# Seven block products instead of eight in the first product of token mixing, for three of four pairs of batches

## The chip, the cores and the metric

The kernel runs on one core of a Trainium2 chip. The core has TensorE (matrix products, written PE in the profile, its weight loads PEld), VectorE (DVE), ScalarE (ACT), GpSimd (POOL) and SyncE (SP, which here only issues DMAs). The engines run side by side, each through its own queue in order, and meet through semaphores. TensorE writes its results to PSUM, a memory of a few banks; everything else lives in SBUF, 128 partitions wide. The metric is the device time of one execution in microseconds (us); lower is better.

## The reference

Eight batches of 576 tokens. First an attention without softmax, then an MLP mixer:

```python
kv  = einsum('bhsd,bhde->...', k, v)          # per head, 64 x 64
o   = q @ kv
x   = o / rms(o) * g_norm                      # (8, 576, 512) after the heads are joined
...
xt  = x.transpose(0, 2, 1)
h   = maximum(xt @ w_tok1, 0) @ w_tok2         # token mixing: 576 -> 256 -> 576
u   = x + h.transpose(0, 2, 1)
out = u + maximum(u @ w_ch1, 0) @ w_ch2        # channel mixing: 512 -> 1536 -> 512
```

All of it is float32. The weights arrive as 64-bit floats and are rounded to 32 bits on the chip ("rounding" below). The change touches `xt @ w_tok1`, the first product of token mixing.

## The kernel before

The batches go in four **pairs**. For each pair the kernel computes attention (five groups of 128-token tiles, `X[pair, 0]` to `X[pair, 4]`: `X[pair, 0]` and `X[pair, 1]` are the 512 first tokens of the first batch, two tiles of 128 x 512 each, `X[pair, 2]` and `X[pair, 3]` those of the second, and `X[pair, 4]` the last 64 tokens of both) and then token mixing. After the last pair comes channel mixing, some 585 us in which seven block products stand for eight at two levels already.

Token mixing of a pair (`token_mixing`, L598) has two products. The first (`tok1`, L601) has four results, one PSUM bank each: `acc[side, t]`, for the two batches `side` of the pair and the two halves `t` of the 256 hidden columns. Each is a sum of four matmuls of 128 x 128 x 512 over the four token tiles, 16 in all, plus a remainder of 64 tokens (`tok1_rem`, L608, four matmuls on half of the array's rows). A ReLU on ScalarE then moves each bank to `h1[side][:, t]`. The second product (`tok2`, L625) makes nine tiles `u0` to `u8`. Where a tile was seeded, ScalarE has copied x into the bank beforehand and copies the sum back; otherwise VectorE adds the bank to x. POOL issues the DMAs that write u to memory.

The order of everything is written by hand as strings of step names (`middle`, `steady`, `last`, from L1385), which `play` (L1317) runs through, and each engine works in that order. Names that matter here:

- `a` attention matmuls, `q` squares (ScalarE), `g` gains (VectorE, from PSUM), `t` sums of squares (VectorE), `m r i` mean, root (ScalarE) and inverse; then x is scaled by `s` on ScalarE (eight small instructions), by `d` on VectorE or by `p` on POOL. Attention is played a pair ahead of mixing; a minus, as in `-d31`, means the pair before that: for attention steps the pair that is being mixed, for `-u8` and `-v8` the pair mixed before.
- `kv`, `e`: the small products k-transposed times v, and their copies.
- `h00` to `h11`: the four sums of `tok1`; `hr`: the remainder and the ReLUs; `z`: seeds; `u0` to `u8`: `tok2`.
- a number: so many rounding steps. A block of channel weights takes two scalings on ScalarE and clamp, shift and add (a custom instruction) on VectorE. In the last pair four sums of `w_ch1` (`mix_ch1`, L292, VectorE, 128 x 1536 each) stand between the fourth and the fifth step (L1442).
- `x`: transposes of finished u tiles on VectorE, `b`: their DMAs; `f`, `l`, `lq`: loads; `o`, `c`, `s`: weights and sums for channel mixing.

PSUM has a pool `h` of four banks, which `tok1`, the seeds and `tok2` take in turn. The tile `h1` has two buffers, so one for each side. The second side's first half of a pair, `X[pair, 3]`, is made last: its attention `a3` runs just before the pair's `tok1`, and its scaling (`-i3 -d31 -s30`) beside it.

The mixing of pair 0 lies in `middle`, of pairs 1 and 2 in `steady`, of pair 3 in `last`; `steady` also holds the attention of the next pair, `last` holds none. In `last` `u0` follows `hr` at once; in the others `a1` and two kv products lie between them.

Of the kernel before, what the change touches and what calls it, by code (L numbers as in the profile page):

```python
# [11 lines left out]
F32 = mybir.dt.float32  # L12
# [3 lines left out]
ALU = mybir.AluOpType  # L16
# [4 lines left out]
def kernel(  # L21
# [32 lines left out]
    nc = tc.nc  # L54
    P = 128
    B, S, DM = k.shape
# [4 lines left out]
    J, JJ, HF, Q = 4, 5, 64, 32  # L61
    LO = P * J
    assert D == 64 and DM == 512 and S == LO + HF and B % 2 == 0
    NC, NF, NTOK = DM // P, DCH // P, DTOK // P
# [6 lines left out]
    NU = B + 1  # L71
    NG = 1 + B // 2
    T = 2 * P
    assert B // 2 == 4
    EPS = 1e-6
    TOP = (2.0 - 2.0 ** -3 - 2.0 ** -23) * 2.0 ** -96

    def pool(name, bufs, side="left", stack=ctx, **kw):
        return stack.enter_context(tc.tile_pool(name=name, bufs=bufs, side=side,
                                                reuse_waits="tile", **kw))  # L80
# [34 lines left out]
    def do(f, *a, **kw):  # L115
        return lambda: f(*a, **kw)

    late = {}
# [4 lines left out]
    def dma(o, i, engine=nc.sync):  # L123
        keep(engine.dma_start(o, i))

    def tensor_add(o, a, b, op=ALU.add, engine=nc.vector):
        keep(engine.tensor_tensor(out=o, in0=a, in1=b, op=op))  # L127

    def relu(o, a):
        keep(nc.scalar.activation(o, a, AF.Relu))  # L130

    def copy(o, a):
        keep(nc.scalar.copy(o, a))  # L133

    def matmul(*a, **kw):
        keep(nc.tensor.matmul(*a, **kw))  # L136
# [120 lines left out]
    def get_ch2(f):  # L257

        def loads(raw):
            t = raw.rearrange("p (f n) w -> p f n w", f=2)  # L260
            rows = words(moe_w_ch2)[ts(f, 2 * P)].rearrange("(f p) n w -> f p n w", f=2)
            return [(t[:, i], rows[i]) for i in range(2)]

        dst = w_ch2[:, 2 * f // NS, ds(2 * f % NS, 2)]
        return block(2 * DM, loads, dst.rearrange("p f h n -> p (f h n)"), True)
# [117 lines left out]
    def x_of(pair, i):  # L383

        return X[pair, i // 2][:, i % 2]
# [209 lines left out]
        return steps  # L595


    def token_mixing(pair, seeds, aside=()):  # L598
        h1, acc = {}, {}

        def tok1(side, t, js=range(J)):  # L601
            if js[0] == 0:
                acc[side, t] = ps["h"].tile([P, DM], F32, name="ps_h", tag="h")
            for j in js:
                matmul(acc[side, t], lhsT=w_tok1[j // 2][:, j % 2, ts(t, P)],
                                 rhs=x_of(pair, side * J + j), start=(j == 0), stop=False)

        def tok1_rem():  # L608
            for t in range(NTOK):
                for side in range(2):  # L610
                    r = ds(side * HF, HF)
                    matmul(acc[side, t], lhsT=w_tok1r[r, ts(t, P)],
                                     rhs=x_of(pair, 8)[r], start=False, stop=True)
            for side in range(2):
                h1[side] = hp_.tile([P, NTOK, DM], F32, name="h1", tag="h1")
                for t in range(NTOK):
                    relu(h1[side][:, t], acc[side, t])

        def seed(i):


            acc[i] = ps["h"].tile([P, DM], F32, name="ps_u", tag="h")
            copy(acc[i], x_of(pair, i))

        def tok2(i):  # L625
            if i not in seeds:
                n = "o" if i in aside else "h"
                acc[i] = ps[n].tile([P, DM], F32, name="ps_u", tag=n)
            first = i not in seeds
            if i < 8:  # L630
                for t in range(NTOK):
                    matmul(acc[i], lhsT=w_tok2[:, t, ts(i % J, P)], rhs=h1[i // J][:, t],
                           start=(first and t == 0), stop=(t == NTOK - 1), skip_group_check=True)
            else:
                for t in range(NTOK):
                    for side in range(2):
                        matmul(acc[i][ds(side * HF, HF)], lhsT=w_tok2[:, t, LO:],
                               rhs=h1[side][:, t],
                               start=(first and t == 0), stop=(t == NTOK - 1), skip_group_check=True)
            x = x_of(pair, i)  # L640
            if first:
                tensor_add(x, acc[i], x)
            else:
                copy(x, acc[i])
            if i == 8:
                dma(u_rest[ts(pair, P)], x, nc.gpsimd)
                for side in range(2):
                    dma(out[2 * pair + side, LO:], x[ds(side * HF, HF)], nc.gpsimd)
            elif i % 2 == 1:
                dma(  # L650
                    u_rows(2 * pair + i // J)[ds((i % J - 1) * P, 2 * P)]
                    .rearrange("(t p) e -> p t e", p=P), X[pair, i // 2], nc.gpsimd)

        steps = {f"h{s}{t}": do(tok1, s, t) for s in range(2) for t in range(NTOK)}
        steps |= {f"h{s}{t}{j}": do(tok1, s, t, (j,)) for s in range(2) for t in range(NTOK) for j in range(J)}
        steps |= {f"z{i}": do(seed, i) for i in seeds}
        return steps | {"hr": tok1_rem} | {f"u{i}": do(tok2, i) for i in range(9)}


    xg, xt, uT = {}, {}, {}  # L660
# [656 lines left out]
    def play(lines, after={}, **stages):  # L1317

        for name in " ".join(lines).split():
            if name.isdigit():
                for _ in range(int(name)):
                    next(stages["rounding"], lambda: None)()
            elif name[0] == "-":
                stages["before"][name[1:]]()
            else:
                next(stages[s][name] for s in ("attention", "mixing", "more")
                     if name in stages.get(s, ()))()
# [3 lines left out]
    tok2 = [get_tok2(t) for t in range(NTOK)]  # L1333
    first_rows = [get_tok1_half(j) for j in range(2)]
    channel = ([get_ch1(c, f) for f in range(2) for c in range(NC)]
               + [get_ch2(f) for f in range(NF // 2)])
    dma(g_row, bass.AP(tensor=g_norm.tensor, offset=g_norm.offset, ap=[[0, 1], list(g_norm.ap[0])]), nc.gpsimd)
    load(0)
    first_rows[0][0]()
# [32 lines left out]
    def spread_g():  # L1372
# [12 lines left out]
    middle = [  # L1385
# [5 lines left out]
    steady = [[  # L1391
# [10 lines left out]

    attentions = [attention(0, ((0,), (1,), (2,), (3,), (4,)))]
    attentions += [attention(p, ((0, 1), (2, 4), (3,))) for p in range(1, B // 2)]
# [16 lines left out]

    more |= {f"j{n}": do(keep_warm, n) for n in (4, 5, 21)}
    more["gs"] = spread_g
    more |= {f"zk{side}{half}": do(spread_k, side, half) for side in range(2) for half in range(2)}
    more |= {f"zz{side}": do(zero_rows, side) for side in range(2)}
    play(start, attention=attentions[0], mixing=mixings[0], more=more)
    play(middle, attention=attentions[1], mixing=mixings[0], before=attentions[0],
         more=more, rounding=rounding)
    for n in range(1, B // 2 - 1):
        play(steady[n - 1], attention=attentions[n + 1], mixing=mixings[n], before=attentions[n] | {"u8": mixings[n - 1]["u8"]},  # L1430
             more=more, rounding=rounding)


# [2 lines left out]
    late["w2"] = pool("sums", 1, "left", once).tile([P, 3, 4, FQ], F32, name="w2")  # L1436
    late["u0"] = pool("u0", 1, "left", once)
    late["sv0"] = pool("sva", 4, "left", once)
    for i in range(2):
        fetch_once(i)  # L1440
    fill = [list(rounding), mix_ch1()]
    woven = fill[0][:4] + fill[1] + fill[0][4:]  # L1442

    last = [
        "h00 -i3 -d31 -s30 2 -d40 2 o0", "h01 2 o1", "h10 2 o3", "h11 2 o2", "hr z2 1 o4", "u0 z3 1 c0", "u1 z4 1 c1 o5", "u2 z5 c2",
        "u3 z6 1 c3 o6", "u4 z7 1", "u5 z8 1", "u6 1 s0", "u7 s1 s2", "u8 s3 s4"]
    parts1 = [f for o in ORDER1 for f in split(1, o)]
    more = {f"c{i}": f for i, f in enumerate(t_sums(lambda n: uT[0][:, SB[n]]))}
# [98 lines left out]
```

## Time and profile before

| | us |
|---|---|
| median of 3 runs (lowest to highest) | 770.39 (770.33 to 770.89) |
| the profiled execution: span from first to last instruction | 768.4 |
| what lies around the span (median less span) | 2.0 |
| PE busy | 762.0 (99%) |
| DVE busy | 644.5 (84%) |
| ACT busy | 279.5 (36%) |
| POOL busy | 112.8 (15%) |

The stages that the change touches, as start and end on TensorE, with the busy time of each engine in them:

| stage | us | PE | DVE | ACT | POOL |
|---|---|---|---|---|---|
| `tok1` and remainder, pair 1 | 70.15 to 87.28 | 17.13 | 16.49 | 8.31 | 2.41 |
| the same, pair 2 | 111.84 to 128.97 | 17.13 | 13.62 | 9.23 | 1.65 |
| the same, pair 3 | 151.19 to 167.04 | 15.85 | 15.33 | 8.78 | 2.40 |
| `tok2`, pair 3 | 167.04 to 182.84 | 15.80 | 14.16 | 10.88 | 3.00 |

The profiled execution has no time of its own beside its span, so the 2.0 us are taken from the median. A line of the timeline reads: start, length (both us), engine, line of the kernel, operation, output and input by the program's names, shape, and how many instructions were merged. A float32 matmul shows as two instructions, one for each of its two passes. What stands in brackets is idle time before the line and who ended it. TensorE's stages of pairs 1 and 2 include one attention group (64 small matmuls, some 1.1 us).

### The profile page before, as it was taken

What the parts mean: (1) busy time and instruction counts of PE and PEld (TensorE: products, weight loads), DVE (VectorE), ACT (ScalarE), POOL (GpSimd) and SP (SyncE); (2) the same over time, 40 slices, a digit from 0 to 9 for tenths busy, and PEclk for the clock granted to TensorE, in tenths of its full rate; (3) what the DMA queues carried; (4) which work ended last, traced back from release to release, by engine and by line L of the source; (5) the groups of instructions that cost most, each with busy time, mean ns of one, the idle gap of its engine ahead of it and who ended that gap; (6) DMA issues with size and microseconds to landing.
All of it is one profiled execution on the core that took longest, in us unless ns stands there. A gap on an engine that the chain in (4) does not pass through costs nothing.

```text
span 768.4 us, 12735 instructions
## 1 busy us (share of the span) xinstructions
PE 762.0 (99%) x4694; PEld 614.3 (80%) x4694; DVE 644.5 (84%) x956; ACT 279.5 (36%) x563; POOL 112.8 (15%) x125
## 2 busy tenths in 40 slices
PE   9999999999999999999999999999999999999997
PEld 8655555446888888888888888888888888888887
DVE  4868886997757779899968989997898997798996
ACT  3656666773210332512234241123352213325221
POOL 1003030204410000002240002042000227000204
PEclk9999999999999999999999999999999999999999
DMA  9999997599798795599998578999659889855679
GB/s 353 374 374 371 367 373 279 177 332 333 245 290 319 288 284 169 168 275 214 224 228 250 152 221 219 262 187 265 193 154 293 160 227 209 200 153 155 153 192 119
DMA packets 137981, 188.28 MB, mean 245 GB/s; under 512 B 48704, under 2 KB 95808, under 8 KB 135872
## 3 DMA queue, kind: packets, MB, share of 16 engines
q1 hardware_dynamic: 102240, 168.72, 69.1%
q0 software_dynamic: 34848, 18.36, 16.1%
q8 instruction: 38, 0.62, 0.3%
q10 hardware_dynamic: 832, 0.39, 0.2%
q14 instruction: 23, 0.19, 0.1%
HBM read 138.28 MB, written 49.15 MB: 244 GB/s over the span
## 4 chain that ended last, share of the span: by engine, by line
PE 96%; DMA 2%; DVE 1%; SPq 0%; ACT 0%; issue 0%; DVEq 0%
PE ps_d L136 28%; PE ps_b L136 19%; PE ps_a L136 19%; PE ps_u L136 8%; PE ps_h L136 8%; PE ps_v L136 5%; PE ps_c L136 3%; PE ps_w L136 2%; PE ps_kv L136 2%; PE ps_o L136 2%; DMA raw<-in_moe_w_tok_dram 1%; DMA v_in<-in_k_dram 1%; PE ps_r L136 0%; DVE x L494 0%; DVE ms L522 0%; DVE w_tok L211 0%
## 5 line engine op out<-in xcount | busy, mean ns | idle before, releaser
L136 PE MATMUL ps_d<-ui,w 128*128 128x256 f32 x504 | 118.6, 379 | 0.0
L136 PEld LDWEIGHTS ps_d<-ui,w 128*128 128x128 f32 x504 | 95.8, 190 | 13.0
L133 ACT COPY ps_d<-ps_a 128x768 f32<-128x768 f32 (+1 forms) x56 | 32.0, 572 | 199.9 <-PE ps_a L136 196.9
L127 DVE TENSOR_TENSOR v<-v,v 128x1536 f32<-128x1536 f32 (+2 forms) x70 | 103.2, 1482 | 0.3
L136 PE MATMUL ps_b<-sv,w 128*128 128x256 f32 x324 | 78.9, 379 | 0.0
L136 PE MATMUL ps_a<-v,w 128*128 128x256 f32 x324 | 78.7, 379 | 0.0
L1266 POOL DMA_DIRECT2D out_dram<-us x24 | 26.8, 1835 | 291.8 <-ACT p L133 286.5
L136 PEld LDWEIGHTS ps_b<-sv,w 128*128 128x128 f32 x324 | 61.2, 190 | 8.9 <-issue 0.6
L136 PEld LDWEIGHTS ps_a<-v,w 128*128 128x128 f32 x324 | 61.6, 190 | 8.4
L136 PE MATMUL ps_u<-h,w_tok 128*128 128x512 f32 (+1 forms) x160 | 64.7, 599 | 0.0
L136 PE MATMUL ps_d<-v,w 128*128 128x256 f32 x258 | 62.7, 379 | 0.0
L130 ACT ACTIVATE v<-v 128x768 f32<-128x768 f32 (+1 forms) x54 | 42.6, 822 | 55.1 <-DVE v L127 52.3
L136 PE MATMUL ps_h<-x,w_tok 128*128 128x512 f32 x128 | 57.6, 600 | 0.7 <-DVE w_tok L211 0.6
L1266 POOL DMA_DIRECT2D out_dram<-r x40 | 41.3, 1926 | 102.0 <-ACT p L133 80.3
L136 PE MATMUL ps_d<-sv,w 128*128 128x256 f32 x228 | 55.4, 379 | 0.0
L136 PEld LDWEIGHTS ps_d<-v,w 128*128 128x128 f32 x258 | 48.9, 190 | 6.6
L136 PEld LDWEIGHTS ps_u<-h,w_tok 128*128 128x128 f32 (+1 forms) x160 | 25.6, 179 | 31.1 <-issue 26.7
L136 PEld LDWEIGHTS ps_d<-sv,w 128*128 128x128 f32 x228 | 43.3, 190 | 5.9
L136 PE MATMUL ps_a<-uT,w 128*128 128x256 f32 x192 | 46.7, 379 | 0.0
L136 PEld LDWEIGHTS ps_h<-x,w_tok 128*128 128x128 f32 x128 | 23.5, 190 | 28.3 <-issue 24.4
L136 PE MATMUL ps_b<-ui,w 128*128 128x256 f32 x168 | 40.8, 379 | 0.0
L136 PEld LDWEIGHTS ps_a<-uT,w 128*128 128x128 f32 x192 | 36.5, 190 | 5.0
(178 smaller groups left out, 1297.7 us busy)
## 6 DMA issues: line engine op xcount, KB each, us to landing
w<-parts SPq DMA_DIRECT2D x168, 384.0 KB
w<-parts SPq DMA_DIRECT2D x56, 192.0 KB
uT<-blocks SPq DMA_DIRECT2D x36, 256.0 KB
k_in<-in_k_dram SPq DMA_DIRECT2D x8, 1024.0 KB
v_in<-in_v_dram SPq DMA_DIRECT2D x8, 1024.0 KB
qT<-in_q_dram SPq DMA_DIRECT2D x8, 1024.0 KB
out_dram<-x POOLq DMA_DIRECT2D x16, 512.0 KB, 6.9
raw<-in_moe_w_ch_dram SPq DMA_DIRECT2D x8, 768.0 KB
```

The source lines that it names most:

```text
L127: keep(engine.tensor_tensor(out=o, in0=a, in1=b, op=op))
L130: keep(nc.scalar.activation(o, a, AF.Relu))
L133: keep(nc.scalar.copy(o, a))
L136: keep(nc.tensor.matmul(*a, **kw))
L1266: keep(nc.gpsimd.dma_start(to, t()[ds(b * Q, Q), at].rearrange("p n l j -> p n (l j)"), accum_op=ALU.add))
```

## The change

For pairs 1, 2 and 3 the four 2 x 2 blocks of the product (two halves of hidden columns by two halves of 512 tokens, times two halves of tokens by two batches) are formed with seven products `p1` to `p7` of two matmuls each, in the scheme of Strassen and Winograd. Pair 0 keeps the eight. The remainder (`hr`) keeps its four matmuls.

- Four sums of `w_tok1` blocks (`mix_tok1`, `y1` to `y4` in `middle`) are made once, on POOL, in a part of `w_ch2`'s place.
- Four sums of x blocks per pair (`t_sum`, `y1` to `y4`; `y11` and `y12` are `y1` of pairs 1 and 2, played earlier) are made on POOL, in two instructions of 128 x 512 each. They lie in `w_ch2`, in `k_in`, in a new tile of the last pair, and in `h1[1]`, which is free until the ReLU.
- The products gather in banks `a`, `b`, `d`, and `e` at the remainder. ScalarE copies bank `a` to `d` in PSUM after `p1`, bank `b` to `h1[0][:, 1]` after `p5` and bank `d` to `h1[0][:, 0]` after `p6`. VectorE adds bank `d` to `h1[0][:, 1]` after `p7`, and banks `e` and `b` to the two halves of `h1[0]` after the remainder. The ReLUs are then two of 512 columns and one of 1024.
- The DMAs of `u8` become a step of their own, `v8`, played after `y2` in `steady` and after `u8` at the end of the second `steady` list; in the last pair they stay in `u8`.
- The blocks of `w_ch2` are rounded in the order 0, 1, 2, 4, 5, 3, since the place of block 3 holds the sums of `w_tok1`. Some rounding steps move between the lines; each list keeps their number.

```diff
+    def spare(pair, n):
+        if pair == NP - 1:
+            if "tx" not in late:
+                late["tx"] = late["tx0"].tile([P, 2, DM], F32, name="tx")
+            return late["tx"]
+        return weight_room[0] if n == 1 or pair == 1 else k_in[0][:, :2]
...
+        b_block = {11: 2, 12: 0, 21: 3, 22: 1}
+
+        def t_sum(n):
+            b = lambda name: X[pair, b_block[name]]
+            if n == 1:
+                txs[1] = spare(pair, 1)
+                o, x, y = txs[1], b(12), b(11)
+            elif n == 2:
+                txs[2] = h1[1] = hp_.tile([P, NTOK, DM], F32, name="h1", tag="h1")
+                o, x, y = txs[2], b(22), txs[1]
+            elif n == 3:
+                txs[3] = spare(pair, 3)
+                o, x, y = txs[3], b(22), b(12)
+            else:
+                o, x, y = txs[2], b(21), txs[2]
+            for j in range(2):
+                tensor_add(o[:, j], x[:, j], y[:, j], ALU.subtract, nc.gpsimd)
...
+        def p1():
+            new_bank("a")
+            product("a", a_block(0, 0), X[pair, b_block[11]], True)
+            new_bank("d")
+            copy(bank["d"], bank["a"])
+        def p5():
+            new_bank("b")
+            product("b", tok_sum(1), txs[1], True)
+            h1[0] = hp_.tile([P, NTOK, DM], F32, name="h1", tag="h1")
+            copy(h1[0][:, 1], bank["b"])
+        def p6():
+            product("d", tok_sum(2), txs[2], False)
+            copy(h1[0][:, 0], bank["d"])
+        def p3():
+            product("b", tok_sum(4), X[pair, b_block[22]], False)
+        def p7():
+            product("d", tok_sum(3), txs[3], False)
+            tensor_add(h1[0][:, 1], bank["d"], h1[0][:, 1])
+        def p2():
+            product("a", a_block(0, 1), X[pair, b_block[21]], False)
+        def p4():
+            product("d", a_block(1, 1), txs[2], False)
+        def p_rem():
+            new_bank("e")
...
+            tensor_add(h1[0][:, 1], bank["e"], h1[0][:, 1])
+            tensor_add(h1[0][:, 0], bank["b"], h1[0][:, 0])
+            relu(h1[1][:, 1], bank["d"])
+            relu(h1[1][:, 0], bank["a"])
+            relu(h1[0], h1[0])
...
-               + [get_ch2(f) for f in range(NF // 2)])
+               + [get_ch2(f) for f in (0, 1, 2, 4, 5, 3)])
...
-        "a0 q00 g01 q01 g00 t00 t01", "u0 f0", "u1 z4", "u2", "a1 q10 g11 q11 g10",
-        "kv10 kv11 e10 e11 t10 t11 m0 r0 lq0", "u3 z6 i0 d00 s01 d11 f1", "u4 l1", "a2 q20 g21 q21 g20",
-        "a4 q40 t20 g41 q41 t21 g40 lr0 lr1", "u5 s10 t40 t41 m2 r2 f2 1", "u6 1 i2 p20 p21 x00", "u7 1 1"]
+        "a0 q00 g01 q01 g00 t00 t01 y1 y2", "u0 f0", "u1 z4", "u2", "a1 q10 g11 q11 g10",
+        "kv10 kv11 e10 e11 t10 t11 m0 r0 lq0 y3 y4", "u3 z6 i0 d00 s01 d11 f1", "u4 l1", "a2 q20 g21 q21 g20",
+        "a4 q40 t20 g41 q41 t21 g40 lr0 lr1", "u5 s10 t40 t41 m2 r2 f2 1", "u6 1 i2 p20 p21 x00 y11", "u7 1 1"]
...
-        "kv00 kv01 e00 e01 -d40 f3", "-u8 -a3 -q30 -g31 -q31 -g30 -t30 -t31 -m3 -r3 -lq1",
-        "h00 -i3 -d31 -s30 l0 b00 1 1", "h01 f4 x01 1", "a0 q00 g01 q01 g00", "h10 t00 t01 b01 x10 1",
-        "h11 1 x11 1", "hr z2 f5 f6", "a1 q10 g11 q11 g10 lq0", "kv10 kv11 e10 e11 t10 t11 m0 r0", "u0 i0 1",
+        "kv00 kv01 e00 e01 -d40 f3", "-u8 y2 -v8 -a3 -q30 -g31 -q31 -g30 -t30 -t31 -m3 -r3 -lq1",
+        "p1 -i3 -d31 -s30 l0 b00 1", "p5 1", "p6 y3 f4 x01 1", "a0 q00 g01 q01 g00", "p3 y4 t00 t01 b01 x10 1",
+        "p7 1 x11", "p2", "p4 1", "hr z2 f5 f6", "a1 q10 g11 q11 g10 lq0", "kv10 kv11 e10 e11 t10 t11 m0 r0", "u0 i0 1",
...
-        "u4 s10 t40 t41 m2 r2 1 f7", "u5 i2 d20 p21 1 1", "u6 1 f8", "u7 1 1 b10 b11"], [
-        "kv00 kv01 e00 e01 -d40 f9", "-u8 -a3 -q30 -g31 -q31 -g30 -t30 -t31 -m3 -r3 -lq1",
+        "u4 s10 t40 t41 m2 r2 1 f7", "u5 i2 d20 p21 y12 1 1", "u6 1 f8", "u7 1 1 b10 b11"], [
+        "kv00 kv01 e00 e01 -d40 f9", "-u8 y2 -v8 -a3 -q30 -g31 -q31 -g30 -t30 -t31 -m3 -r3 -lq1",
-        "h00 -i3 -d31 -s30 x20 1", "h01 x21 1", "a0 q00 g01 q01 g00", "h10 t00 t01 1 1", "h11 f10 1 1", "hr z2",
+        "p1 -i3 -d31 -s30 x20 1", "p5", "p6 y3 x21 1", "a0 q00 g01 q01 g00", "p3 y4 t00 t01 1 1", "p7 f10", "p2 1", "p4 1", "hr z2",
...
-        "u5 i2 d20 p21 1", "u6 1 f12 b20 b21", "u7 1", "a3 q30 g31 q31 g30", "u8 t30 t31 m3 r3 f13"]]
+        "u5 i2 d20 p21 1", "u6 1 f12 b20 b21", "u7 1", "a3 q30 g31 q31 g30", "u8 v8 t30 t31 m3 r3 f13"]]
...
-        "h00 -i3 -d31 -s30 2 -d40 2 o0", "h01 2 o1", "h10 2 o3", "h11 2 o2", "hr z2 1 o4", "u0 z3 1 c0", "u1 z4 1 c1 o5", "u2 z5 c2",
+        "y1 y2 p1 -i3 -d31 -s30 2 -d40", "p5 2", "p6 y3 y4 2 o0", "p3 2 o1", "p7 2 o3", "p2 o2", "p4", "hr z2 1 o4", "u0 z3 1 c0", "u1 z4 1 c1 o5", "u2 z5 c2",
```

More of the change, by code (lines that the diff above doesn't have):

```diff
@@ L73 @@
     T = 2 * P
-    assert B // 2 == 4
+    NP = B // 2
+    assert NP == 4
     EPS = 1e-6
@@ L595, in attention, with tok_sum, mix_tok1 @@
         return steps
+    weight_room = [w_ch2[:, a, :2].rearrange("p s h n -> p s (h n)") for a in range(2)]
+    def spare(pair, n):
[4 more added lines that the diff above has]
+        return weight_room[0] if n == 1 or pair == 1 else k_in[0][:, :2]
+    def tok_sum(n):
+        return weight_room[1].rearrange("p s (g n) -> p (s g) n", n=2 * P)[:, n - 1].rearrange(
+            "p (j n) -> p j n", j=2)
+    def mix_tok1(n):
+        a = lambda m, k: w_tok1[k][:, :, ts(m, P)]
+        x, y, op = {1: (a(1, 0), a(1, 1), ALU.add), 2: (tok_sum(1), a(0, 0), ALU.subtract),
+                    3: (a(0, 0), a(1, 0), ALU.subtract), 4: (a(0, 1), tok_sum(2), ALU.subtract)}[n]
+        tensor_add(tok_sum(n), x, y, op, nc.gpsimd)
     def token_mixing(pair, seeds, aside=()):
@@ L617, in tok1_rem @@
                     relu(h1[side][:, t], acc[side, t])
+        bank, txs = {}, {}
+        a_block = lambda m, k: w_tok1[k][:, :, ts(m, P)]
+        b_block = {11: 2, 12: 0, 21: 3, 22: 1}
[14 more added lines that the diff above has]
+                tensor_add(o[:, j], x[:, j], y[:, j], ALU.subtract, nc.gpsimd)
@@ new lines, in product, with new_bank @@
+        def product(name, lhs, rhs, start):
+            for j in range(2):
+                matmul(bank[name], lhsT=lhs[:, j], rhs=rhs[:, j], start=(start and j == 0),
+                       stop=False, skip_group_check=True)
+        def new_bank(name):
+            bank[name] = ps["h"].tile([P, DM], F32, name="ps_h", tag="h")
+        def p1():
[3 more added lines that the diff above has]
+            copy(bank["d"], bank["a"])
@@ new lines, in p2 @@
+        def p2():
[4 more added lines that the diff above has]
+            new_bank("e")
+            for t, names in ((1, "ed"), (0, "ba")):
+                for side in range(2):
+                    r = ds(side * HF, HF)
+                    matmul(bank[names[side]], lhsT=w_tok1r[r, ts(t, P)], rhs=x_of(pair, 8)[r],
+                           start=(names[side] == "e"), stop=True, skip_group_check=True)
+            tensor_add(h1[0][:, 1], bank["e"], h1[0][:, 1])
[3 more added lines that the diff above has]
+            relu(h1[0], h1[0])
@@ L623, in seed, with put_rest @@
             copy(acc[i], x_of(pair, i))
+        def put_rest():
+            x = x_of(pair, 8)
+            dma(u_rest[ts(pair, P)], x, nc.gpsimd)
+            for side in range(2):
+                dma(out[2 * pair + side, LO:], x[ds(side * HF, HF)], nc.gpsimd)
         def tok2(i):
@@ L645, in tok2 @@
             if i == 8:
-                dma(u_rest[ts(pair, P)], x, nc.gpsimd)
-                for side in range(2):
-                    dma(out[2 * pair + side, LO:], x[ds(side * HF, HF)], nc.gpsimd)
+                if pair == NP - 1:
+                    put_rest()
             elif i % 2 == 1:
@@ L656, in token_mixing @@
         steps |= {f"z{i}": do(seed, i) for i in seeds}
-        return steps | {"hr": tok1_rem} | {f"u{i}": do(tok2, i) for i in range(9)}
+        steps["v8"] = put_rest
+        if pair:
+            steps |= {f"y{n}": do(t_sum, n) for n in range(1, 5)}
+            steps |= {"p1": p1, "p2": p2, "p3": p3, "p4": p4, "p5": p5, "p6": p6, "p7": p7}
+        return steps | {"hr": p_rem if pair else tok1_rem} | {f"u{i}": do(tok2, i) for i in range(9)}
     xg, xt, uT = {}, {}, {}
@@ L1423 @@
     more["gs"] = spread_g
+    more |= {f"y{n}": do(mix_tok1, n) for n in range(1, 5)}
+    more |= {f"y1{p}": mixings[p]["y1"] for p in range(1, NP)}
     more |= {f"zk{side}{half}": do(spread_k, side, half) for side in range(2) for half in range(2)}
@@ L1429 @@
     for n in range(1, B // 2 - 1):
-        play(steady[n - 1], attention=attentions[n + 1], mixing=mixings[n], before=attentions[n] | {"u8": mixings[n - 1]["u8"]},
+        play(steady[n - 1], attention=attentions[n + 1], mixing=mixings[n], before=attentions[n] | {s: mixings[n - 1][s] for s in ("u8", "v8")},
              more=more, rounding=rounding)
@@ L1438 @@
     late["sv0"] = pool("sva", 4, "left", once)
+    late["tx0"] = pool("tx0", 1, "left", once)
     for i in range(2):
```

## The prediction, made before the result was known

> **What bounds the kernel now.** I read the strips of 40 slices, then the chain that ended last, then the timeline of the token-mixing stages, engine by engine. The page:
>
> ```profile
> PE   9999999999999999999999999999999999999997
> ...
> DVE  4868886997757779899968989997898997798996
> ...
> PE 96%; DMA 2%; DVE 1%; SPq 0%; ACT 0%; issue 0%; DVEq 0%
> ```
>
> TensorE is busy in every slice and makes 96% of the chain, so less TensorE work pays at once, if TensorE isn't made to wait instead. VectorE is the second: nearly full where token mixing runs (slices 4 to 10). The timeline of TensorE, last pair of batches:
>
> ```profile
> 151.19 14.00 PE L136 MATMUL ps_h<-x,w_tok 128*128 128x512 f32 x32
> 165.12 1.99 PE L136 MATMUL ps_h<-x,w_tok1r 64*128 64x512 f32 x8
> 167.04 5.42 PE L136 MATMUL ps_u<-h,w_tok 128*128 128x512 f32 x12
> ```
>
> The 16 products of `tok1` show as 32 instructions (two passes each) with no gap; the remainder and `tok2` follow at once. The only cross-engine need in that stretch is x.
>
> **The gain.** 14.00 / 32 = 0.437 us a pass. Seven block products are 14 matmuls instead of 16: 4 passes fewer, 1.75 us a pair, 5.25 us for three pairs. The remainder's matmuls stay.
>
> **What is added**, per pair. On GpSimd (POOL): eight 128x512 subtractions. No such instruction is in the trace. Nearest rows: the 128x512 scaling with a broadcast factor, two in 2.07 us at 68.00, so 1.04 each; the 128x384 sum of two full inputs, 1.00 us, scaled to 512 columns 1.33. I take 1.2, so 9.6 us a pair. On VectorE: three 128x512 additions (0.68 each). On ScalarE: three PSUM copies (0.6) and a ReLU of 1024 columns (1.05, from the 128x1024 copy row) for two ReLUs of 512. Most of all, waits inside the products: the second bank is first a copy of the first; the fourth product (`p4`) may write that bank only when VectorE's addition of `p7` has read it; `u0` needs addition and then ReLU.
>
> **What a POOL sum does to VectorE.** The trace has POOL arithmetic beside VectorE:
>
> ```profile
> 105.91 0.69 DVE L566 TENSOR_TENSOR x<-x,inv 128x512 f32<-128x512 f32 x1
> 105.97 1.55 POOL L570 TENSOR_TENSOR x<-x,inv 128x512 f32<-128x512 f32 x1
> 106.52 1.42 DVE L202 TENSOR_SCALAR w_ch<-w_ch 128x768 f32<-128x768 f32 x1
> ...
> 110.13 0.55 DVE L202 TENSOR_SCALAR w_ch<-w_ch 128x768 f32<-128x768 f32 x1
> ```
>
> The scaling on POOL took 1.55 instead of 1.04: it waited for VectorE's multiply (until 106.60). The clamp behind it took 1.42 instead of 0.55: it waited for POOL. The same at 147.78 (custom add 2.08 instead of 1.22), 69.62 (shift 0.88 instead of 0.56) and around 196 us, where both engines had work queued and took turns. VectorE operations that read PSUM (0.65 at 69.04), and transposes, were not held. So each POOL sum beside SBUF-to-SBUF VectorE work costs VectorE the sum's whole length. [...]
>
> **Last pair, without that hold.** VectorE works in written order. Ahead of `p7`'s addition stand the first four rounding steps, d40 and four sums of w_ch1:
>
> ```profile
> 160.97 1.75 DVE L127 TENSOR_TENSOR w<-w_ch 128x1536 f32<-128x1536 f32 x1
> 162.75 1.76 DVE L127 TENSOR_TENSOR w<-w,w_ch 128x1536 f32<-128x1536 f32 x1
> 164.43 1.75 DVE L127 TENSOR_TENSOR w_ch<-w_ch 128x1536 f32<-128x1536 f32 x1
> 166.10 1.75 DVE L127 TENSOR_TENSOR w<-w_ch,w 128x1536 f32<-128x1536 f32 x1
> 167.77 0.69 DVE L202 TENSOR_SCALAR w_ch<-w_ch 128x1024 f32<-128x1024 f32 x1
> ```
>
> VectorE has no idle there from 155.2 on, and is free for the addition at 167.77 at the earliest; today TensorE is done with `tok1` and remainder by then. The addition ends at 168.45; `p4` 168.45 to 170.2, the remainder to 172.1, one addition to 172.9, the wide ReLU to 174.0: `u0` at 174.0 instead of 167.04, **+7.0**. That contains the saved 1.75. The sums are not later than that: POOL issues the three DMAs of `v8` first (153.76 to 155.41 in the trace), then `y1` to 157.9 (so `p5` starts 5 us late), `y2` to 160.4, `p6`, `p3`, `p7` to 165.7, `p2` to 167.5.
> **With the hold.** From 155.4 POOL has eight sums, VectorE small reciprocal steps and then only SBUF-to-SBUF work. Taking turns, 7.5 of the eight fall ahead of the addition: 7.5 x 1.2 = 9.0 later. **+16.0**.
>
> **First of the three pairs** (70.15 to 87.28). Without the hold: `p1`, `p5` to 73.65. `p6` needs the copy of the bank, which stands on ScalarE behind the root that ends at 75.61: copy to 76.25, `p6` to 78.05, `a0` (1.1) to 79.15. `p3` needs `p5`'s copy, behind the eight scalings that end at 78.66: `p3` from 79.3, `p7` and `p2` to 84.55. VectorE comes to the addition behind the clamp that ends at 84.73: 85.4. `p4`, remainder to 89.1 against 87.28: **+1.8**. With the hold: `y11` on POOL follows `p20 p21` (end 70.07) and holds the custom add and d40; `y2` falls beside PSUM reads and holds nothing; `y3 y4` hold d31, a clamp and a shift. Five times 1.2 = 6.0: **+7.8**.
> **Second** (111.84 to 128.97). The same steps: `p6` from 115.95, `p3` from 118.95, `p2` to 124.2; the addition behind the custom add that ends at 124.90: 125.55; `p4`, remainder to 129.25: **+0.3**. With the hold, two at `y12`, one at `y2`, two at `y3 y4`: 6.0 more, **+6.3**.
> After the remainder `u0` is covered in these two by `a1` and kv (1.1 + 2.5): additions and ReLU take 2.6.
>
> **At nothing:** the sums of w_tok1 (four of 128x256 on POOL) can run at 28 us, beside VectorE's PSUM reads and reductions; if not covered, at most 4 x 0.65 = 2.6. `v8` behind `y2`: nobody reads those rows soon. The order of the w_ch2 blocks: same steps. The seeds wait for ReLUs of banks that are done before `u0`.
>
> **Sum.** 7.8 + 6.3 + 16.0 = 30.1. The profiled span is 768.4; the median of the runs is 770.39, 2.0 more (launch and end). 768.4 + 30.1 + 2.0 = **800.5 us**.
>
> **The clock.** In the last 8.40 us of the trace the granted clock averages 0.96, everywhere else 1.00; TensorE has its last matmul at 763.75. If 0.04 x 8.40 is time at half clock, it fell some 4 us after the last work. With the hold, TensorE is idle some 8 us between `p2` and `p4` of the last pair, and 3 to 5 us at a time in the others. If the clock falls there, `p4` and remainder (3.65 us) take twice the time: 3.65 in one pair, up to 11 in three. [...]
>
> **Rivals.**
> 1. *The forecast*: POOL and VectorE take turns, and the addition behind VectorE's queue is what `p4` waits for. For it: four places in the trace where both happen. About 790 to 806. Chance 0.60.
> 2. *The same and the clock falls*: 804 to 811. [...] 0.17.
> 3. *No hold between the engines for these subtractions*, only the queue orders: 7.0 + 1.8 + 0.3 = 9.1, so 779.5. Against it: the rows above. With sums at 1.04 and half the turns it lies between. 0.16.
> 4. *Faster*: the additions aren't what TensorE waits for, and the removed passes show: 770.4 - 5.25 = 765.1. It decides in the last pair, if VectorE has `p7`'s addition done by the end of `p2`, some 161.7 without waits. Against it: 6.8 us of sums of w_ch1 stand ahead of it in the written order. 0.05; within 0.2% 0.02, if the losses of the last pair come down to the gain of the others.
> 5. *It doesn't do what it says*: the passes of ps_h would then stay at 128 + 32. The code emits 14 + 4 matmuls per pair; I give it nothing of its own.
>
> **Range:** 779 to 811, from rival 3 to rival 2. A run of this kernel tells 0.2% (1.5 us) from no change: faster 0.05, same 0.02, slower 0.93.
>
> **What would show it.** The full-size ps_h passes 128 down to 116. In the last pair `p4` starts with VectorE's addition as its releaser, around 177 (plus what the earlier pairs shift), `p5` with POOL; the custom adds and clamps between show 1.2 us more than before. POOL's 128x512 sums show 1.0 to 1.3 us plus their waits. If VectorE's operations keep their lengths, rival 3 holds. If `p4` is released by TensorE, or by POOL, the queue step is wrong; if `p6` and `p3` aren't released by ScalarE, those of the first two pairs are.

## The result, and the profile after

The changed kernel takes **804.43 us** (median of 4 runs, 802.71 to 805.16) against 770.38 (770.33 to 770.89) for the kernel before on the same chip: a ratio of 1.0436, interval 1.0424 to 1.0448. The prediction said 800.5, slower. The profiled execution took 802.71, with a span of 799.8; it is the fastest of the four, and the section on the clock gives the likely reason why they differ.

In the kernel after, line numbers of the helpers are one higher (L136 is now L137). The strips and the chain of the page, kernel after:

```profile
PE   9997997967999999999999999999999999999997
...
DVE  4878889797676777989996998997888998698996
...
PE 79%; DVE 8%; ACT 2%; issue 1%; SPq 1%; DMA 1%; DVEq 0%; ACTq 0%
```

TensorE has four slices below nine tenths ahead of the last one (4, 7, 9 and 10: the three `tok1` stages), where it had none. The chain, 96% TensorE before, now runs through VectorE and the queues for a part of the way. The passes of `ps_h` at full size went from 128 to 116, as the change promises, so the removed work is really gone.

The three stages, from the first matmul of `tok1` to the first of the remainder (last pair: to the first of `u0`), on TensorE's timeline:

| stage | before | after | more | forecast |
|---|---|---|---|---|
| pair 1, to the remainder | 15.22 | 22.41 | +7.2 | +7.8 |
| pair 2, to the remainder | 15.22 | 21.12 | +5.9 | +6.3 |
| pair 3, to `u0` | 15.85 | 34.24 | +18.4 | +16.0 |

They add up to 31.5; the spans differ by 799.8 - 768.4 = 31.4. Net, all of the time is in these three places. TensorE in the last pair, kernel after:

```profile
164.53 1.98 PE L137 MATMUL ps_h<-x,w_tok 128*128 128x512 f32 x4
170.09 3.29 PE L137 MATMUL ps_h<-tx,w_ch 128*128 128x512 f32 x4 [3.58 <-POOL tx L128]
173.17 2.53 PE L137 MATMUL ps_h<-h,w_ch 128*128 128x512 f32 x4
179.24 3.78 PE L137 MATMUL ps_h<-x,w_ch 128*128 128x512 f32 x4 [3.54 <-ACT h L134]
182.82 2.83 PE L137 MATMUL ps_h<-tx,w_ch 128*128 128x512 f32 x4
185.48 1.88 PE L137 MATMUL ps_h<-x,w_tok 128*128 128x512 f32 x4
191.31 3.54 PE L137 MATMUL ps_h<-h,w_tok 128*128 128x512 f32 x4 [3.95 <-DVE h L128]
194.78 2.06 PE L137 MATMUL ps_h<-x,w_tok1r 64*128 64x512 f32 x8
```

These are `p1`, `p5`, `p6`, `p3`, `p7`, `p2`, `p4` and the remainder. The brackets name the three waits: `p5` for GpSimd's sum, `p3` for ScalarE's copy of `p5`'s bank, `p4` for VectorE's addition of `p7`. `p5`, `p3` and `p4` also take 3.3 to 3.8 us where four passes take 1.88. Why the addition is late, VectorE, then GpSimd, in the same kernel:

```profile
168.79 7.38 DVE L538 SCALAR_TENSOR_TENSOR ms<-ms,inv 128x16 f32<-128x16 f32 x1
176.20 0.17 DVE L540 SCALAR_TENSOR_TENSOR root<-root,ms 128x16 f32<-128x16 f32 x1
...
180.74 1.76 DVE L207 TENSOR_SCALAR w_ch<-w_ch 128x1024 uint32<-128x1024 uint32 x1
...
188.81 1.75 DVE L128 TENSOR_TENSOR w<-w_ch,w 128x1536 f32<-128x1536 f32 x1
190.48 0.68 DVE L128 TENSOR_TENSOR h<-ps_h,h 128x512 f32<-128x512 f32 x1
```

```profile
168.76 2.49 POOL L128 TENSOR_TENSOR tx<-x 128x512 f32<-128x512 f32 x2
171.21 2.48 POOL L128 TENSOR_TENSOR h<-x,tx 128x512 f32<-128x512 f32 x2
173.66 2.47 POOL L128 TENSOR_TENSOR tx<-x 128x512 f32<-128x512 f32 x2
178.80 3.16 POOL L128 TENSOR_TENSOR h<-x,h 128x512 f32<-128x512 f32 x2 [2.67 <-ACT x L558]
```

VectorE's first line is a step of the reciprocal on 16 columns, like the one below it, 0.17 us of work. It lasts 7.38 us, from 168.79 to 176.17, exactly as long as GpSimd runs its first six sums without a break (168.76 to 176.13, 1.245 each). The shift at 180.74 lasts 1.76 instead of 0.69, beside one of the last two sums. The last two VectorE lines are the end of its queue ahead of `p4`: the fourth sum of `w_ch1`, and directly behind it the addition. `p7` had been done since 185.65; the addition waited for its place in the queue.

In pairs 1 and 2 the waits sit elsewhere, at `p6` (two lines) and, as the `a0` matmuls cover most of it, hardly at `p3` (between them):

```profile
78.85 3.65 PE L137 MATMUL ps_h<-h,w_ch 128*128 128x512 f32 x4 [4.10 <-ACT ps_h L134]
...
83.80 1.98 PE L137 MATMUL ps_h<-x,w_ch 128*128 128x512 f32 x4 [0.21 <-ACT h L134]
...
127.31 3.34 PE L137 MATMUL ps_h<-h,w_ch 128*128 128x512 f32 x4 [4.33 <-ACT ps_h L134]
```

`p6` needs the copy of bank `a` to bank `d`, and that stands on ScalarE behind the root, which VectorE's held steps deliver late. `p4` follows with waits of 1.10 and 1.42 for VectorE's addition.

### The profile page after: what moved, and what is told of

The parts are those of the page before. It is cut to its first block, busy times and chain, and to the rows that moved or that the text cites. A ratio compares the mean times of both kernels' runs of the same rounds, so it can differ in the third digit from the quotient of the medians.

```text
span 799.8 us, 12785 instructions
## 1 busy us (share of the span) xinstructions
PE 768.9 (96%) x4682; PEld 615.2 (77%) x4682; DVE 669.8 (84%) x965; ACT 284.1 (36%) x569; POOL 149.2 (19%) x153
## 4 chain that ended last, share of the span: by engine, by line
PE 79%; DVE 8%; ACT 2%; issue 1%; SPq 1%; DMA 1%; DVEq 0%; ACTq 0%
PE ps_d L137 27%; PE ps_b L137 18%; PE ps_a L137 18%; PE ps_v L137 5%; PE ps_u L137 3%; PE ps_c L137 3%; PE ps_w L137 2%; PE ps_h L137 2%; DVE ms L538 1%; DVE ms L523 1%; DVE x L495 1%; ACT x L558 1%; SPq L125 1%; PE ps_kv L137 1%; DVE w_ch L203 1%
## 5 line engine op out<-in xcount | busy, mean ns | idle before, releaser
L137 PE MATMUL ps_d<-ui,w 128*128 128x256 f32 x504 | 118.6, 379 | 0.0
L137 PEld LDWEIGHTS ps_d<-ui,w 128*128 128x128 f32 x504 | 95.9, 190 | 12.9
L137 PE MATMUL ps_b<-sv,w 128*128 128x256 f32 x324 | 78.9, 380 | 0.0
L137 PE MATMUL ps_a<-v,w 128*128 128x256 f32 x324 | 78.8, 379 | 0.0
L137 PEld LDWEIGHTS ps_b<-sv,w 128*128 128x128 f32 x324 | 61.2, 190 | 8.8 <-issue 0.6
L137 PEld LDWEIGHTS ps_a<-v,w 128*128 128x128 f32 x324 | 61.6, 190 | 8.3
L137 PE MATMUL ps_u<-h,w_tok 128*128 128x512 f32 (+1 forms) x160 | 64.7, 599 | 1.9 <-ACT h L131 1.9
L137 PE MATMUL ps_d<-v,w 128*128 128x256 f32 x258 | 62.7, 379 | 0.0
L137 PE MATMUL ps_d<-sv,w 128*128 128x256 f32 x228 | 55.4, 379 | 0.0
L137 PEld LDWEIGHTS ps_d<-v,w 128*128 128x128 f32 x258 | 49.0, 190 | 6.6
L137 PEld LDWEIGHTS ps_u<-h,w_tok 128*128 128x128 f32 (+1 forms) x160 | 25.6, 179 | 33.1 <-issue 26.9
L137 PEld LDWEIGHTS ps_d<-sv,w 128*128 128x128 f32 x228 | 43.4, 190 | 5.9
L137 PE MATMUL ps_a<-uT,w 128*128 128x256 f32 x192 | 46.7, 379 | 0.0
L137 PE MATMUL ps_b<-ui,w 128*128 128x256 f32 x168 | 40.8, 379 | 0.0
L137 PEld LDWEIGHTS ps_a<-uT,w 128*128 128x128 f32 x192 | 36.5, 190 | 4.9
L128 DVE TENSOR_TENSOR v<-ps_b,u 128x768 f32<-128x768 f32 x28 | 26.8, 956 | 15.6 <-PE ps_b L137 12.5
L134 ACT COPY u<-ps_d 128x256 f32<-128x256 f32 (+1 forms) x44 | 23.2, 527 | 43.2 <-PE ps_d L137 43.2
```

## The experiments

**The theory** is the forecast: the sums on GpSimd hold VectorE (some 21 us in all), and the written order of the queues costs the rest, in the last pair through VectorE's addition behind the sums of `w_ch1`. **Rival A**: no hold; the products simply wait for slow sums. **Rival B**: the waits come from the order of products, copies and additions alone, whoever makes the sums. **Rival C**: moving the steps can't win the loss back, since the chain of seven dependent products is itself too long.

Each ratio below is against the kernel before as measured beside that run: 770.33 us for experiments 1 to 4, 770.52 for 5 to 8.

### 1. The sums left out

```diff
-            for j in range(2):
-                tensor_add(o[:, j], x[:, j], y[:, j], ALU.subtract, nc.gpsimd)
+            use[n] = x
...
-            product("b", tok_sum(1), txs[1], True)
+            product("b", tok_sum(1), use[1], True)
```

(and the same for `p6`, `p7` and `p4`, with `use[2]`, `use[3]` and `use[4]`).

> The seven products as in the changed kernel, but the sums of x blocks are left out: p5, p6, p7 and p4 read plain x blocks (X0, X1, X1, X3) instead, so the output is another one. GpSimd does nothing per pair, and no product waits for it; the written order of all other work stays. Theory (GpSimd's sums hold VectorE, about 22 us of the 34; the rest is the written order: ScalarE's copies behind root and scaling, VectorE's addition behind the sums of w_ch1): 768.4 + 1.8 + 0.3 + 7.0 = 777.5 for the span, 779.5 to 783 as a time, the upper end if the clock falls while p4 of the last pair waits. Rival A (the products wait for the sums, VectorE isn't held to an effect): the same time, 779 to 783. Rival B (the written order alone costs it, sums or not): 800 to 805.

Measured: **785.38 us** (784.2 to 786.48), ratio 1.0193 (1.0177 to 1.0208). The stages: +2.5, +0.4 and +11.0 where the forecast without a hold had 1.8, 0.3 and 7.0. So most of the loss goes with the sums, rival B falls, but the remainder is larger than the theory said. The last pair shows why. ScalarE, then TensorE, of this kernel:

```profile
166.75 1.23 ACT L197 ACTIVATE w_ch<-raw 128x512 f32<-128x512 f32 x2 [5.11 <-DMA blocks<-w_ch]
...
169.14 0.57 ACT L134 COPY h<-ps_h 128x512 f32<-128x512 f32 x1
```

```profile
169.76 3.78 PE L137 MATMUL ps_h<-x,w_ch 128*128 128x512 f32 x4 [6.08 <-ACT h L134]
```

The copy of `p6`'s bank stands on ScalarE behind the scaling of a `w_ch2` block, and that scaling waits 5.11 us for a DMA out of `w_ch` (`blocks<-w_ch`). `p7` may overwrite the bank only after the copy, so it starts at 169.76, and `p2` and `p4` follow it. The addition came at 173.65, released by TensorE, not by its own queue. The trace of before has the same wait for that DMA (2.13 us ahead of the scaling at 162.75), with nothing behind it that mattered. The prediction walked through VectorE's and GpSimd's queues in this pair, not through ScalarE's. On VectorE the step that lasted 7.38 us is back to its own length:

```profile
158.45 0.17 DVE L538 SCALAR_TENSOR_TENSOR ms<-ms,inv 128x16 f32<-128x16 f32 x1
```

### 2. The sums made, but read by nobody

Experiment 1 with the `tensor_add` on GpSimd put back, at the same places; the products still read the plain blocks.

> As no_sums (the products read plain x blocks, another output), but GpSimd still makes all eight sums per pair, at the same places of the written order, and nobody reads them. Theory (VectorE is held while GpSimd works): nearly the loss of the changed kernel, 796 to 805, with VectorE's small steps or clamps in the profile held for the length of GpSimd's sums. Rival A (the products wait for the sums): as no_sums, 779 to 783, since no product waits now.

Measured: **804.41 us** (803.45 to 806.29), ratio 1.0443 (1.0425 to 1.0461), the same as the changed kernel. The stages: +6.1, +8.1, +18.2. No product waits for a sum here, and all of the time is back: rival A falls. The sums cost by being there, 804.41 - 785.38 = **19.0 us**, against 21.0 in the forecast; what the lower clock adds is in the 19.0 (granted 0.984 over the profiled run, 0.995 without sums). VectorE, kernel with unread sums:

```profile
170.54 0.25 DVE L537 RECIPROCAL inv<-root 128x16 f32<-128x16 f32 x1 [0.28 <-ACT root L533]
170.83 7.37 DVE L538 SCALAR_TENSOR_TENSOR ms<-ms,inv 128x16 f32<-128x16 f32 x1
178.24 0.17 DVE L540 SCALAR_TENSOR_TENSOR root<-root,ms 128x16 f32<-128x16 f32 x1
```

The 0.17 us instruction is held again, 7.37 us, though no data links it to GpSimd.

### 3. The sums on VectorE

```diff
-                tensor_add(o[:, j], x[:, j], y[:, j], ALU.subtract, nc.gpsimd)
+                tensor_add(o[:, j], x[:, j], y[:, j], ALU.subtract)
```

> The changed kernel, complete, with the sums of x blocks on VectorE instead of GpSimd, at the same places of the written order. Eight sums of some 0.69 us are 5.5 us a pair on VectorE, in place of being held by GpSimd 6 to 9.4 us. Theory: 9.1 for the written order + 3 x 5.5 = 25.6, so 794 for the span and 796 as a time, the last pair better by some 3 us and the first two about the same. Rival A (waits for the sums): the sums are there in half the time, so under 790. Rival B (the written order alone): 800 to 805.

Measured: **797.88 us** (795.48 to 801.15), ratio 1.0356 (1.0322 to 1.039). A sum takes 0.65 us there instead of 1.245, and the step that lasted 7.38 us takes 0.17 (171.59), but the sums use VectorE's own time: pairs 1 and 2 lose the same as on GpSimd (+7.3, +6.0). The last pair loses 11.9 instead of 18.4, 6.5 better where I had expected some 3. Some 2.4 us more came after `u0`. Of these 1.7 are in `tok2`, which takes 17.56 us instead of 15.87 and runs at a granted clock of 0.50 from 193.34 to 196.75; the other 0.7 I can't place. The total lies where the theory had it, and the stages only partly.

### 4. The last pair with eight products

```diff
-        if pair:
+        if 0 < pair < NP - 1:
```

(the first line of `last` as in the kernel before).

> Complete: pairs 1 and 2 with seven products as changed, the last pair with eight as before. From the two profiles, read stage by stage, pair 1 loses 7.2, pair 2 5.9 and the last 18.4 us. If these add: 768.4 + 13.1 = 781.5 for the span, 783 to 784.5 as a time. If the last pair's loss came only from what the earlier pairs left behind in the queues, much less is won back: 790 or more.

Measured: **784.62 us** (784.36 to 784.91), ratio 1.0183 (1.0168 to 1.0198). Pairs 1 and 2 as in the changed kernel (+7.17, +5.93); the last pair's `tok1` is back to its old length, with 1.4 us more between the remainder and `u0`. So the pairs' losses add up, and the last pair carries 804.43 - 784.62 = 19.8 us of the loss.

### 5. VectorE's addition ahead of the sums of w_ch1

The changed kernel, with one line of `last` in another order: the four sums of `w_ch1` (the `2 o0`, `2 o1` ... steps) stand behind the remainder's additions.

```diff
-"p6 y3 y4 2 o0", "p3 2 o1", "p7 2 o3", "p2 o2", "p4", "hr z2 1 o4",
+"p6 y3 y4 o0", "p3 o1", "p7 o3", "p2", "p4", "hr z2 2 2 2 1 o2 o4",
```

> The changed kernel, complete; in the last pair alone the four sums of w_ch1 (1.75 us each) stand behind the remainder's additions instead of ahead of p7's addition. Theory (p4 waits for VectorE's addition behind these sums): p4 starts at the end of p2, 3.9 us earlier, and more of it at full clock: 799 to 801, if VectorE's later backlog costs nothing. If p4 waits for something else (rival A, the sums of x; rival C, the products' own chain): 803 to 805.

Measured: **795.75 us** (795.33 to 796.11), ratio 1.0326 (1.031 to 1.0341); 8.7 better than the changed kernel. VectorE, then TensorE, last pair of this kernel:

```profile
184.20 0.69 DVE L128 TENSOR_TENSOR h<-ps_h,h 128x512 f32<-128x512 f32 x1 [0.73 <-PE ps_h L137]
...
190.15 1.75 DVE L128 TENSOR_TENSOR w<-w_ch 128x1536 f32<-128x1536 f32 x1
```

```profile
183.93 1.88 PE L137 MATMUL ps_h<-x,w_tok 128*128 128x512 f32 x4
185.64 1.88 PE L137 MATMUL ps_h<-h,w_tok 128*128 128x512 f32 x4
```

The addition now waits 0.73 us for TensorE and is done before `p2` ends, so `p4` follows `p2` without a gap. The stage is 7.1 us shorter (27.13 instead of 34.24), and the 6.8 us of sums, now at 190.15, delay nothing that TensorE needs. This is the queue step by itself, and it is shown. The expectation had `p4` 3.9 us earlier; in its stage it starts 5.4 earlier, as `p7` now takes 1.88 us instead of 2.83 and `p3` 3.43 instead of 3.78, and it takes 1.88 itself instead of 3.54. Not all of the 8.7 us is this step: the profiled spans differ by 5.7 (794.1 and 799.8), as `tok2` here loses 1.7 again (17.57 us, clock 0.50 from 192.12 to 195.54). The rest is time around the spans and the changed kernel's profiled run being its fastest.

### 6. TensorE kept busy in the waits

The changed kernel with useless 128x256 matmuls, into a bank that nobody reads, behind `p1`, `p6` and `p2` of the last pair.

```diff
+    def idle_work(n):
+        t = ps["kv"].tile([P, 2, P], F32, name="ps_k", tag="kv").rearrange("p a n -> p (a n)")
+        for _ in range(n):
+            matmul(t, lhsT=w_tok1[0][:, 0, :P], rhs=w_tok1[0][:, 0], start=True, stop=True)
...
-"y1 y2 p1 -i3 -d31 -s30 2 -d40", "p5 2", "p6 y3 y4 2 o0", "p3 2 o1", "p7 2 o3", "p2 o2",
+"y1 y2 p1 k7 -i3 -d31 -s30 2 -d40", "p5 2", "p6 k8 y3 y4 2 o0", "p3 2 o1", "p7 2 o3", "p2 k14 o2",
```

> The changed kernel, complete, with matmuls of no use (128x256, 0.44 us each, into a bank that nobody reads) in the three long waits of the last pair: seven behind p1, eight behind p6, fourteen behind p2, sized to end before the wait does. Theory (half clock after a wait, p4's four passes took 3.54 us instead of 1.88): the granted clock stays 1.0 there, p4 takes 1.9, u0 starts 1.7 us earlier: 801.5 to 803.5. If the passes are slow for another reason, such as what they read: p4 stays at 3.5 and the time at 804 or more.

Measured: **800.11 us** (800.01 to 800.18), ratio 1.0382 (1.0367 to 1.0398): 4.3 under the changed kernel's median, 2.6 under its profiled run; the two profiled spans differ by 1.4 (798.4 and 799.8). More work on TensorE, less time. TensorE, last pair of this kernel:

```profile
185.61 6.21 PE L137 MATMUL ps_k<-w_tok 128*128 128x256 f32 x28
191.66 1.88 PE L137 MATMUL ps_h<-h,w_tok 128*128 128x512 f32 x4
```

`p4` takes 1.88 us instead of 3.54, and the granted clock is 1.00 from 160 to 198 us (0.80 in the last pair's stage of the changed kernel). The runs lie within 0.17 us of each other, the changed kernel's within 2.45. The changed kernel's profiled run has a mean clock of 0.987, its other three 0.980 and spans of 802.3 to 802.6, so its scatter goes with the clock.

### 7. No sums, and the steps in a better order

Experiment 1, with the products `p1`, `p5`, `p6` and their copies ahead of the root and the scalings, `p3` ahead of `a0`, and `p7`'s addition ahead of the rounding and (last pair) of the sums of `w_ch1`. The first `steady` list and `last` (the second list is changed in the same way):

```diff
-"-u8 y2 -v8 -a3 -q30 -g31 -q31 -g30 -t30 -t31 -m3 -r3 -lq1",
-"p1 -i3 -d31 -s30 l0 b00 1", "p5 1", "p6 y3 f4 x01 1", "a0 q00 g01 q01 g00",
-"p3 y4 t00 t01 b01 x10 1", "p7 1 x11", "p2", "p4 1", "hr z2 f5 f6",
+"-u8 y2 -v8 -a3 -q30 -g31 -q31 -g30 p1 p5 p6 -t30 -t31 -m3 -r3 -lq1",
+"p3 -i3 -d31 -s30 l0 b00", "a0 q00 g01 q01 g00 1",
+"y3 y4 p7 1 f4 x01 1 b01", "p2", "p4", "hr z2 t00 t01 x10 1 1 x11 1 f5 f6",
...
-"y1 y2 p1 -i3 -d31 -s30 2 -d40", "p5 2", "p6 y3 y4 2 o0", "p3 2 o1", "p7 2 o3", "p2 o2", "p4", "hr z2 1 o4", "u0 z3 1 c0",
+"y1 y2 p1 p5 p6 -i3 -d31 -s30 -d40 2", "p3 2 o0", "y3 y4 p7", "p2 2 o1 o3", "p4", "hr z2 2 o2 o4", "u0 z3 2 c0",
```

> As no_sums (sums left out, plain x blocks read, another output), and written order changed: p1, p5, p6 and their ScalarE copies stand ahead of the root and of the scalings, p3 ahead of a0, VectorE's addition of p7 ahead of most rounding steps, and in the last pair the four sums of w_ch1 behind p7's addition, two of them behind the remainder's. Theory (what no_sums still loses, 15 us, is written order alone: ScalarE's copies and VectorE's addition): pairs 1 and 2 come out 1 to 1.75 us ahead of the kernel before, the last pair between 1 ahead and 2 behind: 766 to 771. Rival C (the four-bank chain of the seven products itself costs the time, since each product waits for a copy or an addition of the one before): stays near 785.

Measured: **774.8 us** (773.56 to 776.83), ratio 1.0063 (1.0041 to 1.0084). Order wins 10.6 of the 15.0 us that were left without sums, so rival C is mostly wrong, and so is my hope of 766 to 771: even with the sums free of charge the kernel isn't faster in this order. The pairs stand at -1.35, -0.18 and +3.27; 1.75 less each would be the full gain. In the last pair `p6` still waits 2.57 us for the bank copy behind the root, which stays behind it there, and `u0` 1.93 for the wide ReLU. Another 1.1 us came elsewhere (0.5 ahead of pair 1, 0.6 around a seed that ScalarE copies).

### 8. Two pairs, in the better order, with the sums

Experiment 4 (last pair with eight) with pairs 1 and 2 in the order of experiment 7, `p6` behind the root.

> Complete; the last pair with eight products as in last_pair_eight, pairs 1 and 2 in the new order of no_sums_reordered except that p6 stays behind the root, with GpSimd's sums. Theory: the queue waits go, VectorE is still held by the sums: by hand pair 1 is 2.2 us behind the kernel before and pair 2 1.5: 773 to 777, against 784.6 in the old order. If the hold alone makes the loss (order without weight here): 782 to 785.

Measured: **779.65 us** (778.61 to 781.04), ratio 1.0118 (1.0102 to 1.0134): 5.0 under experiment 4, and the best complete version with seven products, still slower than before. It lies between the two expectations: the pairs lose 2.8 and 2.7 (expected 2.2 and 1.5), and 3.6 us come at waits for ScalarE between and behind them (0.9 at a seed between the pairs, 0.4 and 2.3 ahead of `u0` in the last; the 2.3 are its wait for the ReLU on ScalarE).

## Why the prediction was right, point by point

The direction and the mechanism were right; the forecast was 3.9 us, 0.5%, short. That it came so near is partly luck: between the medians the written order cost 15.0 us where 9.1 was forecast, the sums 19.0 where 21.0 was, and the clock, for which the sum has no term, is in both.

- **The gain** (1.75 a pair): the 12 passes are gone. No stage shows a gain, as forecast; `p4` ends later than the sixteenth product did.
- **The hold of VectorE by GpSimd's sums** (forecast 21.0): shown, 19.0 by experiments 1 and 2. The sum was mis-sized by little, 1.245 instead of 1.2 us. The picture of turns was right in places only. In pair 1 two steps of 0.17 us lasted 1.18 each, one sum apiece; in the last pair one such step outlasted six sums. In the last pair VectorE lost 9.4 us in all (7.2 in that step, 1.1 each in the scaling at 179.05 and the shift at 180.74), near the 10.0 that GpSimd's eight sums took.
- **Written order without the hold** (forecast 1.8 + 0.3 + 7.0 = 9.1): experiment 1 has 2.5 + 0.4 + 11.0 = 13.9 in the stages. The step that failed is the last pair's, where the prediction says that VectorE is free "for the addition at 167.77 at the earliest" and counts from there. Without sums the addition came at 173.65, because `p7` itself was late: ScalarE's copy waited behind a scaling that waited for a DMA. In the changed kernel that doesn't show, since VectorE's queue is later still.
- **The last pair with both** (forecast +16.0, measured +18.4): the addition started at 190.48. The forecast's 167.77, moved by the 13.34 us that the stage starts later, is 181.11, so the hold is 9.4 there instead of 9.0. From the addition's start to `u0` it took 8.3 instead of 6.2; 1.7 of these 2.1 us are `p4` at half clock (0.50 from 191.54 to 194.95). The 8 us that the prediction saw TensorE idle between `p2` and `p4` were 3.95: the hold also kept ScalarE's copy ahead of `p3` back, which the prediction hadn't followed, so `p3` waited 3.54 us itself.
- **The clock** (rival 2, 0.17): it did fall, to 0.50, five times in the kernel after (from 78.90, 126.69, 171.06, 177.89 and 191.54 us). In the kernel before it stands at 0.50 from 767.75 us on, 4.0 behind the end of the last matmul, the half that the prediction reckoned with. The prediction gave 3.65 us in one pair up to 11 in three; in the profiled run it is the 1.7 us at `p4` and up to 1.8 and 1.5 at `p6` of the first two pairs, which the waits behind it partly hide. By experiment 6, full clock in the last pair alone is worth 1.4 us of span against the profiled run and some 4 against the three others. So what happened is rival 2, the forecast with the clock falling (804 to 811), at its lower end.
- **The pieces "at nothing"**: the four sums of `w_tok1` ran at 28.02 and 51.30 us, and pair 1 starts 0.08 us later than before. That held.
- **The miss of 3.9 us in terms**: the stages lost 1.4 more than forecast (31.5 against 30.1); the time lay 2.9 us around the profiled span where 2.0 was assumed, 0.9 more; and the median lies 1.7 above the profiled run. That is 4.0, the whole miss to rounding.
- **What would show it**: `p4` released by VectorE's addition, `p5` by GpSimd, `p6` and `p3` of pairs 1 and 2 by ScalarE: as written, except that `p3` of pair 2 didn't wait at all. The custom adds, clamps and shifts that were held show 0.9 to 1.1 us more, not 1.2, the small steps up to 7.2.

Still open: where the other 0.7 us after `u0` of experiment 3 come from. Not tried: seven products with sums that neither VectorE nor GpSimd makes.

## What to carry to other kernels

Removing work from the engine that bounds a kernel pays only if what feeds it keeps pace: 12 removed passes were worth 5.25 us, while the sums that paid for them cost 19.0 by holding another engine, and the new order of products, copies and additions lost some 15 more, the 5.25 already taken off. Ahead of such a change, walk through the queue of every engine that a new dependency crosses (ScalarE too) and ask what stands in front of the instruction and what that in turn waits for, DMAs included. A chain of dependent products needs its small copies and additions early in their queues; that one line of order was worth 8.7 us here between the medians, 5.7 between the profiled spans.

## What the runs showed of the hardware

**The clock went by windows here, not by gaps.** In six of these kernels (after, and experiments 1, 2, 3, 5 and 8), from 60 to 215 us, the granted clock changed only on a grid of 3.41 us (in the kernel after at 78.90, 82.31, 126.69, 130.10, 171.06, 174.47, 177.89, 184.72, 191.54 and 194.95) and was 1.00 or 0.50; a stretch at 0.50 (half clock) lasted one to three such windows. The grid's windows in the last pair of the kernel after (columns: from and to, length, busy PE, PEld, DVE, ACT, POOL, granted clock, DMA share, GB/s):

```profile
167.65:171.06 3.41, 0.97 (x2) 0.30 (x2) 3.06 (x4) 0.70 (x2) 3.39 (x5) 1.00 0.99 344
171.06:174.47 3.41, 3.35 (x5) 1.46 (x5) 3.41 (x1) 0.00 (x0) 3.41 (x4) 0.50 0.98 333
174.47:177.89 3.42, 1.24 (x3) 0.19 (x1) 3.32 (x5) 1.19 (x5) 1.66 (x2) 1.00 0.09 22
177.89:181.30 3.41, 2.06 (x3) 1.02 (x4) 3.41 (x4) 3.38 (x9) 2.50 (x2) 0.50 0.47 123
181.30:184.72 3.42, 3.42 (x6) 1.29 (x5) 3.39 (x3) 3.12 (x6) 0.65 (x1) 0.50 1.05 353
```

PE busy 0.97 of 3.41 us: the next window is at half clock. Busy 3.35: full again. Busy 1.24: half; busy 2.06 of that, at half clock: half once more; busy 3.42: full at 184.72. In the same six kernels every window at full clock with at most 1.28 us busy was followed by half clock, none with 1.74 or more was, and those between (1.42 to 1.57) went either way. At half clock up to 2.06 us kept it, 2.79 and more raised it. So half clock also followed windows that weren't idle throughout: in experiment 8 waits of 0.55 and 1.89 us, 2.2 us of them in one window (1.20 busy), were enough.

```profile
73.00:76.41 3.41, 1.20 (x3) 0.30 (x2) 3.41 (x5) 0.99 (x2) 3.39 (x4) 1.00 1.00 408
76.41:79.82 3.41, 3.17 (x4) 1.52 (x5) 3.03 (x6) 0.82 (x3) 3.40 (x6) 0.50 1.05 413
```

Where the grid falls against the kernel differs between these traces: the first half-clock window starts at 78.90 us in the kernel after and at 76.07 in experiment 5, with `p6` at 78.85 and 78.74. If it differs between runs of one kernel too, that would explain the scatter of the changed kernel; that is an inference, supported by experiment 6, which took the scatter away (0.17 us instead of 2.45).

**An instruction of 0.17 us was held for 7.38 us** by six sums of GpSimd without a break (168.79 in the kernel after, 7.37 with unread sums), while in other places the two engines took turns sum by sum (1.18 us each at 78.54 and 79.75 in the kernel after). Not every hold lies beside a sum: at 77.13 a mean step (L528) takes 0.84 us instead of 0.17 while GpSimd only issues DMAs (76.70 to 78.39), and at 168.01 of the same kernel it takes 0.20 beside such issues (167.10 to 168.75). What decides when a waiting VectorE instruction gets its turn stays open.
